# Attention chunks of 512 and 416 columns, raw loads staged in the pools of the split tiles, and a bucket prefill in halves

## The chip, the cores and the metric

The kernel runs on one core of a Trainium2 chip. The metric is the device time of that core in microseconds (us), lower is better, taken as the median of the runs. Three runs of the kernel before gave 1568.79, 1567.44 and 1567.44 us.

## What is computed

The reference has two stages, with B = 8 batches, S = 1856 rows, D = 256, 16 experts and F = 1024:

```python
scores = np.matmul(z, z.transpose(0, 2, 1)) / S        # z: 8 x 1856 x 64
x = u * np.matmul(np.maximum(scores, 0.0) ** 2, v)     # u, v: 8 x 1856 x 256
g = argmax(x @ w_group); e = argmax(x @ w_expert[g])   # 4 groups of 4 experts
out = softmax_g * softmax_e * (np.maximum(x @ w1[g, e], 0.0) @ w2[g, e])
```

The 14848 rows of x go each through one expert of 16. All is float32 to the outside; the kernel keeps float32 accuracy by splitting each matmul operand into a high and a low part of the type fp32r and adding two or three products.

## The kernel before, in words

**Attention.** For each batch the 1856 query columns are cut into four chunks, `QW` of 480, 480, 448 and 448 columns (L54). A chunk takes 15 steps, one for each 128 rows of keys (the last has 64), so there are 8 x 4 x 15 = 480 steps. In a step `scores` (L265) issues two matmuls (L272, L273) into one of three PSUM banks; ScalarE applies relu (L275) and square (L281, or L278 and L279 in steps 4 and 10); VectorE makes the high part (`ah`, L282) and the low part (`al`, L285). `attn_v` (L291) then adds six matmuls (L302, L303, L305) to two accumulators; the last step has four. Scores run `LEAD` = 5 steps ahead of `attn_v`.

**Loads.** z and v of a batch come in four blocks each. `prep_z` (L206) and `prep_v` (L236) issue the load on SyncE's queue and return a function that splits the block: a ScalarE cast (L218, L253) and a VectorE subtraction (L219, L254). The raw blocks lie in rings of their own with two buffers each (`stg` for v and the expert weights, `zr` for z); the split tiles lie in the pools `vb` (16 buffers of 128x1024) and `q` (26 buffers of 128x512), which also hold `ah` and `al`, the weights, and the hidden tiles. `prep_zm` (L224) builds the moving operand of the scores, the high part of z in 64 partitions and the low part in the other 64, with VectorE copies (L231, L232). Blocks 0 and 1 of batch 0 are loaded at the start, blocks 2 and 3 in steps 0 and 4; those of the next batch at the steps of a table `PREP` (L714), which names for each block the (chunk, step) of its load and of its split.

**Router and buckets.** `chunk_end` (L313) multiplies the accumulators by u, casts to `xh` and `xl`, writes 16-bit planes that SyncE transposes by DMA to rows (L349), and computes the router's logits with four matmuls (L357, L358), whose transpose is a DMA into `lgx` (L365). Eight steps after the end of the chunk `logits_tr` (L369) reads `lgx` on VectorE (L371); from the next step on, but not before step 42, the generator `route` (L399) is advanced by three operations a step: some 27 small VectorE operations, three small matmuls (L452 to L454), and four scatters by GpSimd (L488) that write the rows into a bucket for each expert in device memory. Before that, `prefill` (L687) has filled each expert's bucket with padding rows, one DMA of 1320 KB for each, issued on SyncE's queue at every second step from 10 to 40.

**Experts.** When all chunks are done the rows of each expert come back by transposing loads in blocks of up to 512. Phase 1 (L628 to L630) has 48 matmuls a block, phase 2 (L660, L661) makes the output, which GpSimd scatters (L674). Weights of the next expert but one are loaded in four pieces (`load_w`, L158), two at the start of a block and two behind the first splits.

The order of the instructions on each engine is made by the framework's scheduler from the program order above; a tile takes any free buffer of its pool.

Of the kernel before, what the change touches and what calls it, by code (L numbers as in the profile page):

```python
# [29 lines left out]
def tile_glu_attn_moe(  # L30
# [23 lines left out]
    QW = [480, 480, 448, 448]  # L54
    QO = [0, 480, 960, 1408]
# [10 lines left out]
    LEAD = 5  # L66
    NWARM = 32
# [3 lines left out]
    NEARLY = 2  # L71
    FRZ = min(512, min(caps[:NEARLY]))
# [13 lines left out]
    def new_vb(name):  # L86
        return sb("vb", [P, 1024], F32R, 16, name)

    def new_stg(name):
        return sb("stg", [P, 1024], F32, 2, name)  # L90

    def new_z(name):
        return sb("q", [P, 512], F32R, 26, name)

    def new_rows(name):
        return sb("rows", [P, 4, RW], I32, 3, name)
# [34 lines left out]
    whl = cst("whl", [P, ND, P], F32R)  # L131
    wh0 = cst("wh0", [P, ND, P], F32R)
# [16 lines left out]
    cst("pad", [P, 432])  # L149

    def make_router():
        nc.sync.dma_start(wrs, wr.rearrange("(c p) l -> p c l", p=P))
        for m in (whl, wh0):
            nc.gpsimd.memset(f32(m), 0.0)
            nc.vector.tensor_copy(out=m[:, :, 0:NL], in_=wrs)
        nc.vector.tensor_sub(out=whl[:, :, NL:2 * NL], in0=wrs, in1=f32(whl[:, :, 0:NL]))

    def load_w(e, wt, piece, name):  # L158

        raw = new_stg(f"raw_{name}_{piece}")  # L160
        if piece < 2:
            nc.sync.dma_start(raw, w1[ds(e, 1), piece * P:(piece + 1) * P, :].rearrange("o p f -> p (o f)"))

            def split():
                hi, lo = wt["h"][piece], wt["l"][piece]
                nc.scalar.copy(out=hi, in_=raw)
                nc.vector.tensor_sub(out=lo, in0=raw, in1=f32(hi))
        else:
            q = piece - 2
            rv = raw.rearrange("p (a d) -> p a d", d=D)  # L170
            nc.sync.dma_start(
                rv, w2[ds(e, 1), q * 4 * P:(q + 1) * 4 * P, :].rearrange("o (a p) d -> p (o a) d", p=P)
            )

            def split():
                for j in range(2):
                    t = wt["2"][2 * q + j].rearrange("p (a t d) -> p a t d", a=2, t=2)
                    nc.scalar.copy(out=t[:, :, 0, :], in_=rv[:, 2 * j:2 * j + 2, :])
                    nc.vector.tensor_sub(out=t[:, :, 1, :], in0=rv[:, 2 * j:2 * j + 2, :], in1=f32(t[:, :, 0, :]))

        return split

    def new_w(name):
        h, l = [], []
        for d in range(ND):
            h.append(new_vb(f"w1h_{name}_{d}"))
            l.append(new_vb(f"w1l_{name}_{d}"))
        return {"h": h, "l": l, "2": [new_vb(f"w2_{name}_{q}") for q in range(4)]}
# [17 lines left out]
    def prep_z(b, c):  # L206
# [29 lines left out]
    def prep_v(b, c):  # L236
        n = min(4, NK - 4 * c)
        nfull = min(n, NKF - 4 * c)
        raw = new_stg(f"vr_{b}_{c}")
# [73 lines left out]
    def chunk_end(s):  # L313
# [17 lines left out]
        lgp = sb("zr", [P, 512], F32, 2, f"lgp_{b}_{c}").bitcast(U16)[0:LP].rearrange("p (t h q) -> p t h q", t=4, q=P)  # L331
# [22 lines left out]
        def logits():  # L354
            ps = bank(ps_m, "m", f"pl_{b}_{c}")
            for d in range(ND):
                nc.tensor.matmul(ps[:, 0:w], whl[:, d, :], xh[:, d, 0:w], start=(d == 0), stop=False)  # L357
                nc.tensor.matmul(ps[:, 0:w], wh0[:, d, :], xl[:, d, 0:w], start=False, stop=(d == ND - 1))  # L358
# [22 lines left out]
        defer(s + wait, logits_tr)  # L381
        gens.append((max(s + wait + 1, 42), g))
# [13 lines left out]
    def rt_(tag, shape, name, dt=F32):  # L396
        return sb("rt_" + tag, [P] + shape, dt, 2 if tag in ("lg", "gl", "di") else 1, f"{tag}_{name}")

    def route(b, c, rows, lg, nt, part):  # L399
# [37 lines left out]
        if part:  # L437
            nc.vector.memset(oh16[part:P, nt - 1, :], 0.0)
# [60 lines left out]
    def sort_experts():  # L499
# [4 lines left out]
        sq = lambda name: sb("stg", [P, 1024], F32, 2, name)[:, 0:NE * NE].rearrange("p (a b) -> p a b", b=NE)  # L504
# [182 lines left out]
    def prefill(e):  # L687
        ins = nc.sync.dma_start(
            bucket[e * CAPB:e * CAPB + CMAX, :].rearrange("(p t) w -> p t w", p=P),
            padrow.unsqueeze(1).to_broadcast([P, CMAX // P, RW]),  # L690
# [5 lines left out]
    pz = prep_z(0, 0)  # L696
    pv = prep_v(0, 0)
# [3 lines left out]
    pz1 = prep_z(0, 1)  # L701
    pv1 = prep_v(0, 1)
    pz()
    prep_zm(0, 0)
    pv()
    make_router()
    load_ut(0, 0)
    if B == 1:
# [3 lines left out]
    pv2 = []  # L712
# [6 lines left out]
    for s in range(LEAD):  # L719
        if s == 4:  # L720
            pz1()
        scores(s)
    for s in range(NS):
        b, c, k = steps[s]
        if s == 1:
            pv1()
        if s in (0, 4):
            n0 = s // 4 + 2
            pz1 = prep_z(0, n0)
            pv2.append(prep_v(0, n0))  # L730
        if s in (2, 6):
            pz1()
        if s in (5, 9):
            pv2.pop(0)()
        if b == 0 and s >= 10 and s % 2 == 0 and s < 10 + 2 * NE:
            prefill((s - 10) // 2)
        nxt = s // NK + 1
        if k == 0:
            if nxt < B * NQ:
                load_ut(nxt // NQ, nxt % NQ)  # L740
            if b + 1 == B:
                if c == 0:
                    wts[0] = new_w("e0")
# [43 lines left out]
    for i, (e, r0, n) in enumerate(blocks):  # L787
# [6 lines left out]
        if ld is not None:  # L794
            wts[ld] = new_w(f"e{ld}")
# [27 lines left out]
    def ot(shape, name, dt=F32):  # L823
# [3 lines left out]
        if n == 1024:  # L827
            return new_stg(f"ov_{name}").rearrange("p (a b) -> p a b", b=shape[1])
# [77 lines left out]
    with tc.For_i(0, kreg) as iv:  # L906
        e_ov = nc.sync.value_load(ei[0:1, ds(iv, 1)], min_val=0, max_val=NE - 1)
        wt = new_w("ov")
# [55 lines left out]
```

## Time and profile before

| | |
|---|---|
| median of three runs | 1567.44 us (1567.44 to 1568.79) |
| the profiled execution's own time | 1568.45 us |
| its span, first to last instruction | 1566.7 us |
| TensorE (PE) busy | 1543.9 us, 99% |
| VectorE (DVE) busy | 1107.8 us, 71% |
| ScalarE (ACT) busy | 1000.4 us, 64% |
| mean granted TensorE clock | 0.995 |

Matmuls overlap in the pipeline, so a busy TensorE can still be slower than its best rate. What counts is how many matmuls a stretch holds and how far apart their starts are. Where a row has text in square brackets, it is the idle time of the engine just before the instruction, and what ended it. SPq is the issuing side of SyncE. A PEclk of 1.00 is 2.4 GHz, 0.50 is 1.2 GHz.

### The profile page before, as it was taken

The numbers are of one execution on the slowest core, as the hardware profiler recorded it, in microseconds if no ns is written. First come the engines' busy times: TensorE is split into PE (matmuls) and PEld (weight loads), VectorE is DVE, ScalarE is ACT, GpSimd is POOL, SyncE is SP. The second block draws the span as 40 slices with busy tenths as digits, with TensorE's granted clock in tenths as the row PEclk, the third lists the DMA queues.
The fourth block names the chain that finished last, engine by engine and source line by source line (L and its number), as shares of the span: only waits on it lengthen the run. The fifth ranks groups of instructions, "written<-read, shape, count | busy, mean of one in ns | idle before, by whom it ended". The sixth has DMA issues, their size and how long they took to land. (4 is left out here: it accounts for less than half of the span.)

```text
span 1566.7 us, 23639 instructions
## 1 busy us (share of the span) xinstructions
PE 1543.9 (99%) x7760; PEld 1343.0 (86%) x7760; DVE 1107.8 (71%) x2705; ACT 1000.4 (64%) x1932; POOL 293.4 (19%) x376
## 2 busy tenths in 40 slices
PE   7999999999999999999999999999999999999998
PEld 6887888888988988888889898998888888888887
DVE  6869788888788887887888656555555555555672
ACT  6877878787888887878787445444444444444432
POOL 0003212121212121212112211111221211111111
PEclk9999999999999999999999999999999999999999
DMA  8994334252443241423144344324433333433200
GB/s 252 326 272 116 88 77 107 56 137 55 99 101 87 78 112 51 109 57 96 47 113 106 100 117 126 83 82 101 107 103 96 92 104 102 96 101 103 61 21 21
DMA packets 250541, 162.83 MB, mean 104 GB/s; under 512 B 174232, under 2 KB 235676, under 8 KB 250416
## 3 DMA queue, kind: packets, MB, share of 16 engines
q1 hardware_dynamic: 238480, 130.40, 33.0%
q0 software_dynamic: 11936, 30.90, 6.1%
q8 instruction: 61, 1.00, 0.3%
q14 instruction: 64, 0.52, 0.1%
HBM read 72.50 MB, written 53.61 MB: 80 GB/s over the span
## 5 line engine op out<-in xcount | busy, mean ns | idle before, releaser
L302 PE MATMUL o<-ah,vl 128*128 128x448 f32 (+1 forms) x960 | 361.1, 376 | 3.1 <-DVE ah L282 2.4
L303 PE MATMUL o<-ah,vh 128*128 128x448 f32 (+1 forms) x960 | 359.9, 375 | 0.0
L660 PE MATMUL py<-w_e,hh 128*128 128x512 f32 x976 | 332.1, 394 | 0.0
L275 ACT ACTIVATE r<-sc 128x480 f32<-128x480 f32 (+1 forms) x480 | 259.0, 554 | 110.7 <-PE sc L273 74.6
L285 DVE TENSOR_TENSOR al<-r,ah 128x480 fp32r<-128x480 f32 (+1 forms) x448 | 285.0, 636 | 42.6 <-ACT r L279 21.3
L305 PE MATMUL o<-al,vh 128*128 128x480 f32 (+1 forms) x896 | 291.5, 377 | 5.3 <-DVE al L285 5.2
L639 DVE SCALAR_TENSOR_TENSOR hl<-ph,hh 128x512 fp32r<-128x512 f32 (+5 forms) x288 | 172.1, 605 | 114.3 <-ACT hh L633 106.4
L661 PE MATMUL py<-w_e,hl 128*128 128x256 f32 x976 | 251.9, 280 | 0.0
L633 ACT ACTIVATE hh<-ph 128x512 fp32r<-128x512 f32 (+7 forms) x288 | 153.5, 540 | 147.2 <-PE ph L630 139.4
L281 ACT ACTIVATE r<-r 128x480 f32<-128x480 f32 (+1 forms) x416 | 239.6, 591 | 5.0
L674 POOL DMA_INDIRECT out_dram<-y,meta x128 | 128.2, 1001 | 545.9 <-DVE y L672 521.6
L488 POOL DMA_INDIRECT bucket<-rows,di x128 | 136.8, 1069 | 401.3 <-DVE di L467 338.4
L628 PE MATMUL ph<-xh_m,w1l_e 128*128 128x512 f32 (+7 forms) x576 | 207.8, 361 | 0.7 <-DVE hl L639 0.7
L629 PE MATMUL ph<-xh_m,w1h_e 128*128 128x512 f32 (+7 forms) x576 | 207.8, 361 | 0.0
L630 PE MATMUL ph<-xl_m,w1h_e 128*128 128x512 f32 (+7 forms) x576 | 206.3, 361 | 0.0
L302 PEld LDWEIGHTS o<-ah,vl 128*128 128x128 f32 x960 | 181.3, 189 | 28.1 <-DVE ah L282 4.8
L660 PEld LDWEIGHTS py<-w_e,hh 128*128 128x128 f32 x976 | 175.2, 187 | 32.8
L303 PEld LDWEIGHTS o<-ah,vh 128*128 128x128 f32 x960 | 181.3, 189 | 21.2
L305 PEld LDWEIGHTS o<-al,vh 128*128 128x128 f32 x896 | 167.5, 189 | 29.6 <-DVE al L285 10.1
L282 DVE CAST ah<-r 128x480 fp32r<-128x480 f32 (+1 forms) x416 | 166.0, 401 | 35.5 <-ACT r L281 29.4
L661 PEld LDWEIGHTS py<-w_e,hl 128*128 128x128 f32 x976 | 181.5, 188 | 10.7
L272 PE MATMUL sc<-zm,z2h 128*128 128x480 f32 (+1 forms) x480 | 181.7, 381 | 3.9 <-ACT r L275 2.4
(146 smaller groups left out, 1891.6 us busy)
## 6 DMA issues: line engine op xcount, KB each, us to landing
raw_e<-in_w_dram SPq DMA_DIRECT2D x64, 512.0 KB
bucket<-padrow SPq DMA_DIRECT2D x16, 1320.0 KB
vr<-in_v_dram SPq DMA_DIRECT2D x24, 512.0 KB
ut<-in_uT_dram SPq DMA_DIRECT2D x16, 480.0 KB
ut<-in_uT_dram SPq DMA_DIRECT2D x16, 448.0 KB
zr<-in_zT_dram SPq DMA_DIRECT2D x48, 128.0 KB
vr<-in_v_dram SPq DMA_DIRECT2D x8, 256.0 KB
rows<-pl SPq DMA_TRANSPOSE x128
```

Of the source, the lines that this page charges most:

```text
L272: nc.tensor.matmul(ps[:, 0:w], z2h[:, ks], zm, start=True, stop=False)
L275: nc.scalar.activation(out=a, in_=ps[:, 0:w], func=AF.Relu, scale=1.0 / S)
L281: nc.scalar.activation(out=a, in_=a, func=AF.Square)
L285: nc.vector.tensor_sub(out=al, in0=a, in1=f32(ah))
L302: nc.tensor.matmul(o, vl[:, dsl], ah, start=(k == 0), stop=False)
L303: nc.tensor.matmul(o, vh[:, dsl], ah, start=False, stop=(k == NK - 1))
L305: nc.tensor.matmul(o, vh[:, dsl], al, start=False, stop=False)
L628: nc.tensor.matmul(o, wt["l"][d][:, fs], xh[:, d, 0:W], start=(d == 0), stop=False)
L629: nc.tensor.matmul(o, wt["h"][d][:, fs], xh[:, d, 0:W], start=False, stop=False)
L630: nc.tensor.matmul(o, wt["h"][d][:, fs], xl[:, d, 0:W], start=False, stop=(d == ND - 1))
L660: nc.tensor.matmul(py[0:m], hh[:, ts], w2t, start=(f == 0), stop=False)
L661: nc.tensor.matmul(py[0:m, 0:D], hl_[:, ts], w2t[:, 0:D], start=False, stop=(f == NF - 1))
```

## The change

Chunks get 512, 512, 416 and 416 columns. Raw blocks of z are staged in the pool `q` (27 buffers), raw v and weights in `vb` (18 buffers), so that the rings `stg` and `zr` go; `lgp` gets a buffer of its own, `rows` a fourth, `lgx` three. All z and v loads of batch 0 are issued at the start, the second half of the first z block on ScalarE's queue; for that block the operand of the scores is made directly from the raw block, half by ScalarE and half by VectorE. The router's weights are loaded at the start and split at step 8, in tiles of 48 columns, not 128. `LEAD` becomes 6, the warm-up has 40 matmuls, not 32. The prefill has 32 DMAs of half the size at steps 8 to 54, one every step and a half (`PFILL`), and routing starts at step 56 with `logits_tr` inside the generator. `PREP` splits v earlier and z later. All four pieces of an expert's weights are loaded at the start of a block.

```diff
-    QW = [480, 480, 448, 448]
-    QO = [0, 480, 960, 1408]
+    QW = [512, 512, 416, 416]
+    QO = [0, 512, 1024, 1440]
...
-    LEAD = 5
-    NWARM = 32
+    LEAD = 6
+    NWARM = 40
...
+    PFILL = [8 + 3 * i // 2 for i in range(2 * NE)]
...
-        return sb("vb", [P, 1024], F32R, 16, name)
-
-    def new_stg(name):
-        return sb("stg", [P, 1024], F32, 2, name)
+        return sb("vb", [P, 1024], F32R, 18, name)
+
+    def new_vraw(name):
+        return sb("vb", [P, 1024], F32, 18, name)
+
+    def new_zraw(name):
+        return sb("q", [P, 512], F32, 27, name)
...
-        return sb("rows", [P, 4, RW], I32, 3, name)
+        return sb("rows", [P, 4, RW], I32, 4, name)
...
-    whl = cst("whl", [P, ND, P], F32R)
-    wh0 = cst("wh0", [P, ND, P], F32R)
+    whl = cst("whl", [P, ND, LP], F32R)
+    wh0 = cst("wh0", [P, ND, LP], F32R)
...
-        zr = sb("zr", [P, 512], F32, 2, f"zr_{b}_{c}")
+        zr = new_zraw(f"zr_{b}_{c}")
         for h in range(2):
-            nc.sync.dma_start(zr[h * DQ:(h + 1) * DQ, 0:w], zT[b, :, q0:q0 + w])
+            eng = nc.scalar if first and h else nc.sync
+            eng.dma_start(zr[h * DQ:(h + 1) * DQ, 0:w], zT[b, :, q0:q0 + w])
...
+            if first:
+                zm = sb("zm", [P, 512], F32R, 2, f"zm_{b}_{c}")
+                nc.vector.tensor_sub(out=zm[DQ:P, :], in0=zr[DQ:P, :], in1=f32(z2h[DQ:P, :]))
+                nc.scalar.copy(out=zm[0:DQ, :], in_=zr[0:DQ, :])
+                zms[(b, c)] = zm
...
-        lgp = sb("zr", [P, 512], F32, 2, f"lgp_{b}_{c}").bitcast(U16)[0:LP].rearrange("p (t h q) -> p t h q", t=4, q=P)
+        lgp = sb("lgp", [P, 512], F32, 1, f"lgp_{b}_{c}").bitcast(U16)[0:LP].rearrange("p (t h q) -> p t h q", t=4, q=P)
...
-        defer(s + wait, logits_tr)
-        gens.append((max(s + wait + 1, 42), g))
+        def late():
+            logits_tr()
+            yield
+            yield from g
+
+        gens.append((max(s + wait, PFILL[-1] + 2), late()))
...
-            nc.vector.memset(oh16[part:P, nt - 1, :], 0.0)
+            if part < 64:
+                nc.vector.memset(oh16[part:64, nt - 1, :], 0.0)
+            nc.vector.memset(oh16[max(part, 64):P, nt - 1, :], 0.0)
...
-    def prefill(e):
+    def prefill(i):
+        r0, n = i // 2 * CAPB + i % 2 * (CMAX // 2), CMAX // 2
...
-        ("v", 0, (0, 1), (0, 7)), ("v", 1, (0, 9), (1, 3)), ("v", 2, (1, 5), (1, 10)), ("v", 3, (1, 12), (2, 4)),
-        ("z", 0, (1, 6), (1, 12)), ("z", 1, (2, 6), (2, 12)), ("z", 2, (3, 5), (3, 11)), ("z", 3, (3, 6), (3, 13)),
+        ("v", 0, (0, 1), (0, 6)), ("v", 1, (0, 7), (0, 12)), ("v", 2, (0, 13), (1, 4)), ("v", 3, (1, 5), (1, 10)),
+        ("z", 0, (2, 4), (2, 12)), ("z", 1, (2, 13), (3, 6)), ("z", 2, (3, 2), (3, 10)), ("z", 3, (3, 6), (3, 14)),
...
-            sp = [load_w(regs(ld)[0], wts[ld], pc, f"e{ld}") for pc in range(2)]
+            sp = [load_w(regs(ld)[0], wts[ld], pc, f"e{ld}") for pc in range(4)]
...
-                sp.append(load_w(regs(ld)[0], wts[ld], (f - 3) // 2 + 2, f"e{ld}"))
```

## Rows read from the trace of the kernel before

**Rows 1.** The page, part 1: the span, and busy time by engine.

```profile
span 1566.7 us, 23639 instructions
PE 1543.9 (99%) x7760; PEld 1343.0 (86%) x7760; DVE 1107.8 (71%) x2705; ACT 1000.4 (64%) x1932; POOL 293.4 (19%) x376
```

**Rows 2.** Windows of 50 us: length, busy time (x instructions) by engine, PEclk, DMA share, GB/s.

```profile
0.00:50.00 50.00, 41.76 (x184) 33.22 (x185) 34.81 (x67) 34.60 (x62) 3.28 (x28) 0.93 0.89 273
50.00:100.00 50.00, 50.00 (x239) 44.48 (x238) 36.21 (x97) 37.70 (x77) 1.35 (x4) 1.00 1.11 303
100.00:150.00 50.00, 46.37 (x209) 37.47 (x208) 40.79 (x131) 40.53 (x80) 13.89 (x19) 0.97 0.70 181
150.00:200.00 50.00, 50.00 (x241) 43.56 (x240) 38.88 (x110) 39.81 (x82) 10.35 (x14) 1.00 0.31 69
200.00:250.00 50.00, 48.67 (x233) 41.50 (x232) 41.17 (x115) 41.47 (x83) 10.52 (x13) 1.00 0.44 112
300.00:350.00 50.00, 50.00 (x246) 44.23 (x245) 41.91 (x120) 42.50 (x86) 7.62 (x13) 1.00 0.38 100
```

**Rows 3.** Waits, whole span: who waited for what, us in total, times, longest.

```profile
DVE lgf L371 <- DMA lgx<-lgp: 40.4, 28, 3.9
...
PE o L305 <- DVE al L285: 5.2, 8, 1.6
```

**Rows 4.** Windows of the head, cut where the granted clock changes; columns as in rows 2.

```profile
5.30:22.40 17.10, 11.66 (x44) 7.64 (x44) 11.37 (x23) 12.25 (x22) 0.00 (x0) 1.00 0.75 218
22.40:29.20 6.80, 6.06 (x15) 5.08 (x16) 5.36 (x9) 2.89 (x4) 0.08 (x1) 0.50 0.96 289
```

**Rows 5.** Timeline of the head and around 120 us: start, length, engine, line, operation.

```profile
0.81 1.22 SPq L211 DMA_DIRECT2D zr<-in_zT_dram  x2
...
1.32 3.59 PE L700 MATMUL warm_ps<-ones 128*128 128x128 bf16 x32 [1.32 <-POOL ones L114]
...
4.08 0.62 ACT L218 CAST z2h<-zr 128x512 fp32r<-128x512 f32 x1 [1.78 <-DMA zr<-in_zT_dram]
...
6.41 0.46 PE L272 MATMUL sc<-zm,z2h 128*128 128x480 f32 x1 [1.50 <-DVE zm L232]
...
9.12 8.59 SPq L241 DMA_DIRECT2D vr<-in_v_dram  x3
...
10.27 0.49 PE L302 MATMUL o<-ah,vl 128*128 128x480 f32 x1 [1.22 <-DVE ah L282]
...
14.99 1.05 ACT L253 CAST vh<-vr 128x1024 fp32r<-128x1024 f32 x1 [2.40 <-DMA vr<-in_v_dram]
...
23.14 1.17 PE L305 MATMUL o<-al,vh 128*128 128x480 f32 x2 [1.49 <-DVE al L285]
...
120.73 0.67 PE L305 MATMUL o<-al,vh 128*128 128x448 f32 x2 [1.60 <-DVE al L285]
```

**Rows 6.** Timeline of TensorE: first and last of steady rows, 448, 512, 352 columns.

```profile
300.92 0.36 PE L303 MATMUL o<-ah,vh 128*128 128x448 f32 x1
...
302.54 0.37 PE L303 MATMUL o<-ah,vh 128*128 128x448 f32 x1
...
1107.08 0.40 PE L629 MATMUL ph<-xh_m,w1h_e 128*128 128x512 f32 x1
...
1109.84 0.39 PE L629 MATMUL ph<-xh_m,w1h_e 128*128 128x512 f32 x1
...
1548.00 0.32 PE L628 MATMUL ph<-xh_m,w1l_e 128*128 128x352 f32 x1
...
1550.26 0.32 PE L630 MATMUL ph<-xl_m,w1h_e 128*128 128x352 f32 x1
```

**Rows 7.** Line 688, the prefill: SyncE's issue in ns (min/median/max), first and last start.

```profile
L688 SPq DMA_DIRECT2D bucket<-padrow x16: 588/872/4495, 22.1 to 95.8; - x16
```

**Rows 8.** Groups by shape: VectorE's two operations of a step at 448 columns.

```profile
L285 DVE TENSOR_TENSOR al<-r,ah 128x448 fp32r<-128x448 f32 x224 | 138.8, 620 | 26.5 <-ACT r L279 12.9 <-ACT r L275 4.7 <-ACT r L281 3.8
...
L282 DVE CAST ah<-r 128x448 fp32r<-128x448 f32 x208 | 82.1, 395 | 12.8 <-ACT r L281 11.8 <-issue 0.4
```

More of the change, by code (lines that the diff above doesn't have):

```diff
@@ L148, in tile_glu_attn_moe, with wr_in @@
     warm = cst("warm", [P, 1])
-    cst("pad", [P, 432])
+    cst("pad", [P, 240])
+    def wr_in():
+        nc.sync.dma_start(wrs, wr.rearrange("(c p) l -> p c l", p=P))
     def make_router():
-        nc.sync.dma_start(wrs, wr.rearrange("(c p) l -> p c l", p=P))
         for m in (whl, wh0):
@@ L158, in load_w, with split, new_w @@
     def load_w(e, wt, piece, name):
-        raw = new_stg(f"raw_{name}_{piece}")
+        raw = new_vraw(f"raw_{name}_{piece}")
+        rv = raw.rearrange("p (a d) -> p a d", d=D)
         if piece < 2:
             nc.sync.dma_start(raw, w1[ds(e, 1), piece * P:(piece + 1) * P, :].rearrange("o p f -> p (o f)"))
-            def split():
-                hi, lo = wt["h"][piece], wt["l"][piece]
+        else:
+            a0 = 4 * (piece - 2)
+            nc.sync.dma_start(rv, w2[ds(e, 1), a0 * P:(a0 + 4) * P, :].rearrange("o (a p) d -> p (o a) d", p=P))
+        def split():
+            if piece < 2:
+                hi, lo = new_vb(f"w1h_{name}_{piece}"), new_vb(f"w1l_{name}_{piece}")
+                wt["h"].append(hi)
+                wt["l"].append(lo)
                 nc.scalar.copy(out=hi, in_=raw)
                 nc.vector.tensor_sub(out=lo, in0=raw, in1=f32(hi))
[L168 to L179, printed above, removed]
-        return split
[L183 to L188, printed above, removed]
+                return
+            for j in range(2):
+                t2 = new_vb(f"w2_{name}_{2 * (piece - 2) + j}")
+                wt["2"].append(t2)
+                t = t2.rearrange("p (a t d) -> p a t d", a=2, t=2)
+                nc.scalar.copy(out=t[:, :, 0, :], in_=rv[:, 2 * j:2 * j + 2, :])
+                nc.vector.tensor_sub(out=t[:, :, 1, :], in0=rv[:, 2 * j:2 * j + 2, :], in1=f32(t[:, :, 0, :]))
+        return split
+    def new_w():
+        return {"h": [], "l": [], "2": []}
     deferred = []
@@ L238, in prep_v @@
         nfull = min(n, NKF - 4 * c)
-        raw = new_stg(f"vr_{b}_{c}")
+        raw = new_vraw(f"vr_{b}_{c}")
         rv = raw.rearrange("p (k d) -> p k d", d=D)
@@ L356, in logits @@
             for d in range(ND):
-                nc.tensor.matmul(ps[:, 0:w], whl[:, d, :], xh[:, d, 0:w], start=(d == 0), stop=False)
-                nc.tensor.matmul(ps[:, 0:w], wh0[:, d, :], xl[:, d, 0:w], start=False, stop=(d == ND - 1))
+                nc.tensor.matmul(ps[0:LP, 0:w], whl[:, d, :], xh[:, d, 0:w], start=(d == 0), stop=False)
+                nc.tensor.matmul(ps[0:LP, 0:w], wh0[:, d, :], xl[:, d, 0:w], start=False, stop=(d == ND - 1))
             for t0, t1, q in ((0, w // P, P), (w // P, nt, part)):
@@ L695, in tile_glu_attn_moe @@
     nc.scalar.activation(out=warm, in_=warm, func=AF.Exp)
-    pz = prep_z(0, 0)
-    pv = prep_v(0, 0)
+    pz, pv = [prep_z(0, 0, first=True)], [prep_v(0, 0)]
     wps = bank(ps_m, "m", "warm_ps")
@@ L700, in tile_glu_attn_moe @@
         nc.tensor.matmul(wps[:, 0:P], ones, ones, start=True, stop=True)
[L701 to L706, printed above, removed]
+    for c in range(1, NQ):
+        pz.append(prep_z(0, c))
+        pv.append(prep_v(0, c))
+        if c == 1:
+            wr_in()
+    pz.pop(0)()
     load_ut(0, 0)
@@ L719, in tile_glu_attn_moe @@
     for s in range(LEAD):
+        if s == 1:
+            pv.pop(0)()
         if s == 4:
-            pz1()
+            pz.pop(0)()
         scores(s)
@@ L725, in tile_glu_attn_moe @@
         if s == 1:
[L726 to L730, printed above, removed]
+            pv.pop(0)()
         if s in (2, 6):
-            pz1()
+            pz.pop(0)()
         if s in (5, 9):
-            pv2.pop(0)()
-        if b == 0 and s >= 10 and s % 2 == 0 and s < 10 + 2 * NE:
-            prefill((s - 10) // 2)
+            pv.pop(0)()
+        if s == 8:
+            make_router()
+        for i in range(2 * NE):
+            if PFILL[i] == s:
+                prefill(i)
         nxt = s // NK + 1
```

22 lines of the change are left out of this document (11 added, 11 removed).

## The prediction

> **What bounds the kernel now.** I read the page first. TensorE is busy for 1543.9 of 1566.7 us [rows 1], so it is the bound, and a faster VectorE or ScalarE is worth nothing unless TensorE waits for it. But a busy share hides a slow clock and small gaps, so I then cut the span into windows of 50 us and read how many matmuls each holds [rows 2]. Steady attention has 241 and 246; the first window has 184, of which 32 are the warm-up [rows 5]; 100 to 150 us has 209, and 200 to 250 us has 233. So time is lost in three places, all in the first 250 us, and what is left of the attention stage and all of the expert stage run without a gap that I could take out. The list of waits says the same: in sum the matmul that reads `al` waits for VectorE for 5.2 us in 8 places, which is the longest entry of TensorE [rows 3]. Third I read the head in windows cut where the granted clock changes [rows 4] and in its timeline [rows 5].
>
> **A matmul's price.** From first to last start there are 8 intervals in 1.62 us at 448 columns, 12 in 2.76 us at 512, 14 in 2.26 us at 352 [rows 6]: 0.2025, 0.230 and 0.161 us. They lie on a line of 0.00043 us a column. On it 480 columns cost 0.216 us and 416 cost 0.189 us.
>
> **The head, as it is.** In 0 to 50 us the 152 matmuls behind the warm-up are worth 152 x 0.216 = 32.9 us; 17.1 us are lost. Of these
> - 6.4 us lie before the first score, which starts at 6.41 [rows 5].
> - From 6.41 to the first `attn_v` at 10.27 are eight score matmuls, 1.7 us; 2.1 us are lost.
> - 5.30 to 22.40 holds 44 matmuls [rows 4], so 36 from 10.27 on, worth 7.8 of 12.1 us; 4.3 us are lost. SyncE stands in a load of v from 9.12 for 8.59 us, since the two raw buffers are full; ScalarE waits 2.40 us for a block of v at 14.99, and behind that wait stands the split of z block 1, which the next scores need [rows 5].
> - 22.40 to 29.20 is at a granted clock of 0.50, the 1.2 GHz level, after TensorE had idled again and again from 6 us on; 15 matmuls are worth 3.2 of 6.8 us [rows 4], 3.6 us are lost, the wait of 1.49 us for `al` at 23.14 among them [rows 5].
> - 0.7 us behind that.
>
> **The change, part by part.**
>
> *Widths.* Each chunk keeps its 118 attention and 4 router matmuls. A wide and a narrow one cost 0.230 + 0.189 = 0.419 us, today's pair 0.216 + 0.2025 = 0.419 us. Cost 0. The 352-column row lies on the line, so no floor stands at 416. On ScalarE and VectorE counts stay and the columns sum to the same; a chunk of 512 needs one plane copy for each half where 480 needs two. Cost 0, gain hidden.
>
> *All first loads at once.* This takes away the block of 8.59 us on SyncE and the wait of 2.40 us behind it. Blocks of z and v are then issued in the order of their use, each some 0.6 us of issue (1.22 us for two, [rows 5]), all eight by about 11 us; the last are wanted at step 9. What is late next is ScalarE and VectorE: until then ten steps of at most 1.0 us each (VectorE, below) and some 5 us of splits stand against ten steps of 8 x 0.230 = 1.84 us, 15 against 18 us, so they keep up on the mean, though not at each step. So I take out most of 4.3 and, as TensorE no longer idles in pieces, most of the 3.6 us: 6.5 us. Bounds: 2 us (the splits still collide) and 8.6 us (all, with the 0.7).
>
> *First operand direct, ScalarE's queue, warm-up, LEAD.* The operand is ready one VectorE operation after the cast, not three, which is up to 0.9 us earlier; the second half of z, issued on another queue, may land 0.6 us earlier, or up to 0.9 us later if it queues behind ScalarE's table load. Eight more warm-up matmuls of 3.59/32 = 0.11 us [rows 5] end at 5.8 us, so the first score can't start before. With a sixth step of scores ahead, ScalarE has one more relu before the steady order. Gain 0.5 us for start, 0.5 for the rest; bounds -1 and 2. Head together: -7.5 us, bounds -1 and -10.6.
>
> *Prefill in 32 halves.* Now 16 DMAs, 21.6 MB, are asked for in steps 10 to 40, some 52 us, and are still being issued at 95.8 us [rows 7]; 50 to 100 us moves 303 GB/s [rows 2], so the rings are full and every load of z and v queues behind padding; SyncE itself stands up to 4.5 us in one issue [rows 7]. Halves every 1.5 steps, 2.6 us, ask for 676 KB/2.6 us = 260 GB/s, under that rate, and end at step 54, about 105 us. On SyncE 32 issues of 0.59 (the least) to 0.87 us (the median) cost 19 to 28 us where 16 cost 14; the transposes for rows and logits are queued behind them, which no one needs before step 56. Cost on the path 0.
>
> *Routing from step 56, `lgp` and more buffers.* In 100 to 150 us 32 matmuls are missing, 32 x 50/241 = 6.6 us; one wait there is for `al` at 120.73, 1.60 us [rows 5], and the clock falls again (0.97 in the mean). VectorE is held in order by `lgf`, which waits for the transpose of the logits: 40.4 us in 28 waits, up to 3.9 us [rows 3]; behind it stand `ah` and `al`, and TensorE waits for those. For the first chunks that transpose has long landed when routing starts at 56. The same 27 small operations for each of the first chunks come later by 14 steps, again at three a step, until about step 110; so VectorE is as full as now, with TensorE one step better buffered. Gain 5 us, bounds 0 and 6.6. From step 110 on `lgf` comes eight steps behind the chunk as before, and waits as before.
>
> *200 to 250 us.* Missing are 8 matmuls, 1.7 us [rows 2]; the longer lead should cover more than half. Gain 1 us, bounds -4 (a loss, by more of such waits in the narrow chunks) and 1.7.
>
> *At no cost.* Weight pieces all at the start of a block, router tiles of 48 columns, the second memset of VectorE in narrow chunks (one less in wide ones), two pools for raw tiles: hidden under a TensorE that doesn't wait; if the pools were full, a load would stand in SyncE as at 9.12 us now. By count `vb` needs 16 + 2 of 18, `q` at most 25 of 27.
>
> **The sum.** The profiled execution took 1568.45 us. Less 7.5, 5 and 1 is 1554.95. It stands 1.0 us over the median of 1567.44, within the spread of the three runs. Forecast: 1555 us; its own range is 1549.5 to 1560.5.
>
> **Rivals.**
> 1. *The head is mended, the middle isn't.* Routing at three operations a step meets the splits of the next batch's v in steps 66 to 85, and VectorE's pile-up only moves. For it: the demand is unchanged. Against it: the late loads are gone. 1568.45 - 7.5 = 1561 us. Chance 0.18.
> 2. *Stalls move in the head too.* ScalarE, not the loads, spaces the first steps; only 2 us are gained: 1566.5 us. For it: ScalarE and VectorE are busy over 11 of the 17 us from 5.3 on [rows 4]. Against it: its longest idle time there is a wait for a load. Chance 0.10.
> 3. *Halves are slow.* If halves moved only 218 GB/s, as the first 17 us did [rows 4], 21.6 MB would take 99 us, not the 83 us of the schedule; loads and transposes would queue 16 us late as today, and the 5 us, the 1 us and some 4 of the head's 7.5 would not come: 1565 us. The Trainium skill speaks for this one: DMA: Bandwidth & Descriptors, Rules for kernel authors, wants at least 1 MiB in a DMA for full bandwidth, and halves have 0.64. The trace shows no prefill of that size, so it neither agrees nor differs. Chance 0.05.
> 4. *Narrow chunks become VectorE's.* A step of 448 columns costs VectorE 0.620 + 0.395 = 1.015 us [rows 8], 15.2 us a chunk; it is busy 41.9 of 50 us [rows 2], so 20.4 of a chunk's 24.3, 5.2 of them not by step. At 416 columns TensorE needs 15 x 8 x 0.189 = 22.7 us; VectorE at most the same 20.4, and with 1.4 us of the `lgf` wait 21.8, which is 96%. With three splits of z put into the last narrow chunk it can pass 22.7, from where each further operation is on the path. At 1.0 us in each of 16 narrow chunks the loss is 16 us: 1568.45 - 13.5 + 16 = 1571 us, slower. Against it: VectorE's time falls with the columns, and wide chunks have 27.6 us for it to catch up. Chance 0.12.
>
> **Chances and range.** The forecast has 0.55. Measurement can tell about 0.2%, 3.1 us, from no change. Faster: the forecast, rival 1, and the better end of rival 2, 0.76. Same: the rest of 2 and rival 3, 0.12. Slower: rival 4, 0.12. The range of 1549 to 1566.5 holds all but rival 4 and the ends.
>
> **What would show it.** Right: about 40.4/0.230 = 175 matmuls behind the 40 warm-ups in 0 to 50 us, where there are 152 now; no SyncE block near 9 us; a granted clock of 1.00 from 6 us on; starts 0.230 and 0.189 us apart; the prefill ending near 105 us. A window of 50 us wholly in wide chunks holds 217 matmuls, one in narrow chunks 264. Wrong: a new row of waits for `al` in the narrow chunks, windows beyond 250 us that stay five or more under what their widths give, or a clock at 0.50 in the head.

## The result

The changed kernel is slower. Its median is 1587.82 us (four runs, 1586.04 to 1591.96) beside 1567.97 us (four runs, 1567.44 to 1568.79) for the kernel before: ratio 1.013, 95% interval 1.0109 to 1.0151. Predicted was 1555 us, between 1549 and 1566.5. The profiled execution took 1588.44 us, 20.0 us more than that of before.

The page of the changed kernel, parts 1 and 5: the span, busy time by engine, and one of TensorE's groups with the idle time ahead of it.

```profile
span 1586.7 us, 23447 instructions
PE 1547.3 (98%) x7768; PEld 1335.2 (84%) x7768; DVE 1100.5 (69%) x2672; ACT 997.0 (63%) x1885; POOL 300.2 (19%) x344
...
L316 PE MATMUL o<-al,vh 128*128 128x512 f32 (+1 forms) x896 | 292.0, 377 | 12.1 <-DVE al L296 11.7
```

VectorE and ScalarE have fewer instructions and less busy time than in [rows 1], and TensorE has eight more, the warm-up. So none of the three got more work that matters. TensorE waits more: 39.4 us of the span are not busy, 22.8 before. Where, is told by windows again: a stretch is worth the matmuls that it holds. The changed kernel (columns as in rows 2):

```profile
0.00:50.00 50.00, 36.81 (x149) 26.42 (x150) 26.94 (x47) 27.84 (x47) 2.48 (x26) 0.86 0.98 302
...
100.00:150.00 50.00, 45.48 (x213) 40.51 (x212) 35.44 (x87) 36.69 (x75) 0.48 (x2) 0.93 0.96 274
150.00:800.00 650.00, 638.07 (x3041) 544.03 (x3041) 528.11 (x1523) 524.04 (x1008) 138.25 (x159) 0.99 0.32 86
```

And the kernel before in the long stretch:

```profile
150.00:800.00 650.00, 648.11 (x3102) 564.17 (x3101) 536.88 (x1549) 533.65 (x1061) 127.74 (x174) 1.00 0.34 85
```

Before 150 us the changed kernel has 149 + 239 + 213 less 40 warm-ups, 561 matmuls, where the kernel before has 600 [rows 2]; from 150 to 800 us it has 3041 against 3102. At 650/3102 = 0.21 us each, 39 and 61 matmuls are 8.2 and 12.8 us, together 21: the 20 us, as nearly as counts tell. Behind 800 us both kernels take 0.190 us a matmul, so the expert stage loses nothing.

Part of the loss is the clock. In the mean of 0 to 50, 100 to 150 and 200 to 250 us the granted clock is 0.86, 0.93 and 0.93, in the kernel before 0.93, 0.97 and 1.00 [rows 2]. The third window of the changed kernel:

```profile
200.00:250.00 50.00, 47.98 (x237) 43.81 (x236) 38.49 (x117) 38.28 (x77) 11.84 (x15) 0.93 0.43 115
```

That is 50 x (0.14 + 0.07 + 0.07) = 14 us of full clock lost against 5, so up to 9 of the 20 us. This is an estimate from these rows, and an upper bound, since an idle TensorE loses nothing to its clock.

Three places stand out in the trace.

**The head.** Timeline of the changed kernel, from 10 us:

```profile
10.57 0.18 DVE L162 CAST whl<-wrs 128x40 fp32r<-128x40 f32 x1 [7.91 <-DMA wrs<-in_wr_dram]
...
10.88 0.69 DVE L227 TENSOR_TENSOR zm<-zr,z2h 64x512 fp32r<-64x512 f32 x1
...
11.62 1.65 PE L283 MATMUL sc<-zm,z2h 128*128 128x512 f32 x3 [5.86 <-DVE zm L227]
```

The first score starts at 11.62 us, at 6.41 before [rows 5]. VectorE stood for 7.91 us ahead of the first operation on the router's weights, and `zm`, which TensorE needs, is behind it. The code asks for that operation at step 8; the scheduler put it first. Why it did so is not shown: the load itself is issued at 4.15 us, and in the kernel before at 4.53 us, where `zm` comes first all the same. The three matmuls of 1.65 us run at the pace of half the clock (starts some 0.46 us apart, 0.228 is the price in experiment 8), and the granted clock of the first 50 us is 0.86. The Trainium skill (Perfetto Trace Analysis, Tensor Engine Instruction (MATMUL, LD_WEIGHTS)) calls VectorE and ScalarE strict first-in first-out; the rows agree: `zm` starts only when the router's operation has run.

**Around 119 us.** Waits of the changed kernel from 100 to 150 us, and its SyncE queue there:

```profile
DVE lgf L382 <- DMA lgx<-lgp: 7.0, 1, 7.0
...
PE o L316 <- DVE al L296: 4.0, 1, 4.0
```

```profile
96.99 7.48 SPq L708 DMA_DIRECT2D bucket<-padrow  x6
...
110.68 8.95 SPq L360 DMA_TRANSPOSE rows<-pl  x4
119.73 1.20 SPq L376 DMA_TRANSPOSE lgx<-lgp  x1
```

`lgf` holds VectorE for 7.0 us, because the transpose of the logits is issued only at 119.73, behind halves of the prefill and four transposes that took 8.95 us. The last half of the prefill is issued at 132.6 us, not at 105:

```profile
L708 SPq DMA_DIRECT2D bucket<-padrow x32: 588/1088/2602, 15.3 to 132.6; - x32
```

**Every batch turn**, where one batch follows another: the first product with v of batches 3, 4 and 5 starts at 246, 354 and 461 us. Two windows of the changed kernel at such a turn:

```profile
250.00:300.00 50.00, 48.04 (x210) 37.31 (x209) 37.99 (x112) 39.59 (x72) 9.92 (x10) 1.00 0.26 66
...
450.00:500.00 50.00, 47.99 (x213) 37.12 (x213) 41.78 (x116) 41.23 (x75) 8.93 (x9) 1.00 0.32 91
```

TensorE is idle for 2 us of each, with a clock of 1.00, and so at 350 and 550 us (209 and 218 matmuls); the kernel before has no idle time in three of these four and 0.2 us in the one from 550. From 200 to 250 us there are another 2 us, and behind a wait of 1.8 us at 238 us the clock falls (the 0.93 above). SyncE's waits of line 252, the load of v, in 200 to 800 us, in the changed kernel:

```profile
SPq L252 <- PE o L314: 26.1, 4, 9.6
...
SPq L252 <- PE o L316: 13.8, 5, 3.2
SPq L252 <- PE sc L284: 4.4, 4, 1.2
```

and of the same load in the kernel before:

```profile
SPq L241 <- DVE vl L254: 20.7, 7, 6.8
```

Before, a load of v mostly waits until a raw block has been split. Now it waits for a matmul, 44 us in 13 waits. L314 and L316 read the split tiles of v, so the slot, a buffer of the pool, that the load needs holds a split tile which TensorE still reads (L284 reads none of them; its 4.4 us are only put down to it). So blocks land late, and ScalarE stands for them; its waits from 200 to 800 us:

```profile
ACT vh L264 <- DMA vr<-in_v_dram: 9.4, 9, 1.3
```

The kernel before has no such wait there. What ScalarE does for TensorE is behind it in order. TensorE's waits from 150 to 800 us, in the changed kernel:

```profile
PE sc L283 <- ACT r L286: 6.1, 9, 1.8
PE o L316 <- DVE al L296: 4.9, 12, 0.6
```

and in the kernel before:

```profile
PE o L305 <- DVE al L285: 1.6, 4, 0.6
```

The splits also come closer together. ScalarE's splits of v at one turn, changed kernel:

```profile
450.89 1.05 ACT L264 CAST vh<-vr 128x1024 fp32r<-128x1024 f32 x1 [0.34 <-DMA vr<-in_v_dram]
...
454.21 1.05 ACT L264 CAST vh<-vr 128x1024 fp32r<-128x1024 f32 x1
...
458.93 0.83 ACT L264 CAST vh<-vr 128x768 fp32r<-128x768 f32 x1
...
465.42 1.05 ACT L264 CAST vh<-vr 128x1024 fp32r<-128x1024 f32 x1 [1.23 <-DMA vr<-in_v_dram]
```

The first three of these are 3.3 and 4.7 us apart; before the fourth, ScalarE stands for 1.23 us, and TensorE's waits of this turn follow it, from 469 to 477 us. In the kernel before:

```profile
425.51 1.05 ACT L253 CAST vh<-vr 128x1024 fp32r<-128x1024 f32 x1
...
432.90 1.04 ACT L253 CAST vh<-vr 128x1024 fp32r<-128x1024 f32 x1
```

The next two start at 439.4 and 445.8 us. The four are 6.4 to 7.4 us apart, three of them ahead of the turn at 445.0 us.

### The profile page after: what moved, and what is told of

It is laid out like the page before. It is cut to its first block, busy times and chain, and to the rows that moved or that the text cites. A ratio compares the mean times of both kernels' runs of the same rounds, so it can differ in the third digit from the quotient of the medians.

```text
span 1586.7 us, 23447 instructions
## 1 busy us (share of the span) xinstructions
PE 1547.3 (98%) x7768; PEld 1335.2 (84%) x7768; DVE 1100.5 (69%) x2672; ACT 997.0 (63%) x1885; POOL 300.2 (19%) x344
## 5 line engine op out<-in xcount | busy, mean ns | idle before, releaser
L313 PE MATMUL o<-ah,vl 128*128 128x416 f32 (+1 forms) x960 | 361.4, 377 | 5.3 <-DVE ah L293 4.5
L314 PE MATMUL o<-ah,vh 128*128 128x416 f32 (+1 forms) x960 | 358.5, 373 | 0.0
L286 ACT ACTIVATE r<-sc 128x512 f32<-128x512 f32 (+1 forms) x480 | 259.0, 554 | 129.8 <-PE sc L284 81.9
L296 DVE TENSOR_TENSOR al<-r,ah 128x512 fp32r<-128x512 f32 (+1 forms) x448 | 286.3, 639 | 33.5 <-ACT r L290 23.7
L316 PE MATMUL o<-al,vh 128*128 128x512 f32 (+1 forms) x896 | 292.0, 377 | 12.1 <-DVE al L296 11.7
L507 POOL DMA_INDIRECT bucket<-rows,di x128 | 142.9, 1116 | 531.1 <-DVE di L486 393.8
L292 ACT ACTIVATE r<-r 128x512 f32<-128x512 f32 (+1 forms) x416 | 238.9, 592 | 5.0
L693 POOL DMA_INDIRECT out_dram<-y,meta x128 | 133.8, 1046 | 535.4 <-DVE y L691 507.5
L316 PEld LDWEIGHTS o<-al,vh 128*128 128x128 f32 x896 | 167.5, 190 | 40.7 <-DVE al L296 20.4
L314 PEld LDWEIGHTS o<-ah,vh 128*128 128x128 f32 x960 | 182.2, 190 | 19.7
L293 DVE CAST ah<-r 128x512 fp32r<-128x512 f32 (+1 forms) x416 | 167.6, 406 | 41.8 <-ACT r L292 41.2
L283 PE MATMUL sc<-zm,z2h 128*128 128x512 f32 (+1 forms) x480 | 182.7, 384 | 13.0 <-ACT r L286 7.0
```

The costliest lines, as they stand in the source:

```text
L283: nc.tensor.matmul(ps[:, 0:w], z2h[:, ks], zm, start=True, stop=False)
L286: nc.scalar.activation(out=a, in_=ps[:, 0:w], func=AF.Relu, scale=1.0 / S)
L292: nc.scalar.activation(out=a, in_=a, func=AF.Square)
L296: nc.vector.tensor_sub(out=al, in0=a, in1=f32(ah))
L313: nc.tensor.matmul(o, vl[:, dsl], ah, start=(k == 0), stop=False)
L314: nc.tensor.matmul(o, vh[:, dsl], ah, start=False, stop=(k == NK - 1))
```

## The experiments

Each was timed beside the kernel before; medians of that were 1568.3 to 1568.7 us. The theory was that **slots** are scarce, since raw blocks lie in the pools of the split tiles. Rivals: **narrow chunks** fall behind VectorE (rival 4 of the prediction), and the **head**.

### 1. The router's weights loaded beside their split

```diff
-        if c == 1:
-            wr_in()
...
+            wr_in()
             make_router()
```

> The changed kernel with the load of the router's weights moved from the start to step 8, beside their split. Theory H (at the start VectorE holds the first operand and the low part of z behind the router's split, which waits for its small load until 10.6 us): the first score starts at 5.5 to 6.5 us, not at 11.6, and the time falls by 4 to 8 us, to 1580 to 1584; the windows behind 200 us keep their losses. Rival (the head is bound by the first loads of z and v, all asked for at once): the first score still starts behind 9 us, and the time stays within 2 us of 1588.

1594.17 us, ratio 1.0168 (1.015 to 1.0186): worse, outside of both expectations. Timeline:

```profile
6.12 0.99 PE L283 MATMUL sc<-zm,z2h 128*128 128x512 f32 x3 [0.36 <-DVE zm L227]
...
13.13 0.79 PE L313 MATMUL o<-ah,vl 128*128 128x512 f32 x1 [4.32 <-DVE ah L293]
...
20.72 0.18 DVE L162 CAST whl<-wrs 128x40 fp32r<-128x40 f32 x1 [3.87 <-DMA wrs<-in_wr_dram]
```

The first score starts at 6.12, as the theory of the head wanted, but the first product with v only at 13.13 (10.27 before, 16.91 in the changed kernel): ScalarE stands for 2.41 us for the second block of v, and the scores' work is behind that split. The router's load, issued at 14.58 us behind the first loads of z, v and u, holds VectorE at 20.72. The first 50 us hold 144 matmuls, where the changed kernel has 149. Mending one such wait uncovers the next.

### 2. The widths of before in the changed kernel

```diff
-    QW = [512, 512, 416, 416]
+    QW = [480, 480, 448, 448]
```

> The changed kernel with chunks of 480, 480, 448, 448 columns, all else kept. Theory W (rival 4 of the prediction, narrow chunks leave VectorE too little time): the waits for al at the turn of each batch go, 12 to 17 us come back, 1571 to 1576. Theory S (raw blocks in the pools of the split tiles make the splits of v wait and then come in a heap at the turn): the heap stays, 1585 to 1591.

1587.63 us, 1.012 (1.0103 to 1.0137): no difference from the changed kernel. TensorE is idle for 11.7 us from 150 to 800 us, 11.9 in the changed kernel, and waits of 1.3 to 1.4 us for `al` stand at 254, 361, 469 and 577 us. So the narrow chunks of rival 4 don't make the stalls at the turns.

### 3. Rings of their own for the raw tiles

```diff
-        return sb("vb", [P, 1024], F32, 18, name)
+        return sb("stg", [P, 1024], F32, 2, name)
...
-        return sb("q", [P, 512], F32, 27, name)
+        return sb("zr", [P, 512], F32, 2, name)
...
-        lgp = sb("lgp", [P, 512], F32, 1, f"lgp_{b}_{c}")...
+        lgp = sb("zr", [P, 512], F32, 2, f"lgp_{b}_{c}")...
```

> The changed kernel with raw blocks in rings of their own again (two buffers for v and weights, two for z, shared with the logits' planes; vb 16, q 26). Theory S: the splits of v spread over some 12 steps before the turn of a batch, as in the kernel before; each turn from batch 2 on loses under 1.5 us where it now loses about 4; 10 to 15 us come back, 1573 to 1578, with the head still near 21 us lost. Theory W: the turns keep their losses, 1585 to 1591.

1572.89 us, 1.0029 (1.0017 to 1.004): 14.9 us back with nothing else undone. `q` and `vb` have 26 and 16 buffers again. Its long window:

```profile
150.00:800.00 650.00, 644.71 (x3102) 554.59 (x3101) 538.74 (x1554) 535.80 (x1024) 132.20 (x160) 1.00 0.32 86
```

61 matmuls more than the changed kernel, 12.8 of the 14.9 us; ScalarE never stands there for a block of v to land; and line 252 waits no more for a matmul; its longest entry is

```profile
SPq L252 <- DVE vl L265: 9.4, 8, 1.5
```

The head changes too, though nothing of its loads was touched. Timeline:

```profile
5.11 0.69 DVE L227 TENSOR_TENSOR zm<-zr,z2h 64x512 fp32r<-64x512 f32 x1 [2.45 <-ACT z2h L224]
...
9.91 0.18 DVE L162 CAST whl<-wrs 128x40 fp32r<-128x40 f32 x1 [0.49 <-DMA wrs<-in_wr_dram]
```

The router's operation is behind `zm` again, and the first score starts at 5.86 us. So it stood first only with the shared pools and all first loads together; with the shared pools alone (experiment 10) `zm` starts at 6.16 us and the router's operation at 9.54.

The experiment gives back both pools and the logits' planes at once. By SyncE's waits it is `vb` that matters: in the changed kernel line 217, the load of z, waits for 7 us from 200 to 800 us, line 252 for 44.

### 4. The preparation steps of before in the changed kernel

The two lines of `PREP` as in the kernel before.

> The changed kernel with the table of load and split steps of the kernel before. Theory S: the splits of z spread over the batch again, those of v stay in a heap since the pool lets none go earlier; 2 to 6 us come back, 1582 to 1586. Theory T (the table alone makes the heap): the turns lose no more than before, 10 to 15 us come back, 1573 to 1578.

1582.6 us, 1.0092 (1.0076 to 1.0109): 5.2 us back. Loads of v and splits are spread wider in this table, and line 252 waits 32 us for matmuls, not 44.

### 5. Both: rings and preparation steps

> The changed kernel with pools of its own for the raw tiles (as in the run with split pools) and with the order of preparation steps of before; widths, first loads, prefill and routing stay as changed. If the lack of free slots is what bunched the splits at each batch turn, both edits mend the same thing and do not add: 1568 to 1573 us, about the 1572.9 of the pools alone. If the order of the steps has a cost of its own, they add: 1567 to 1569 us (1587.8 - 15 - 5). Against it, what remains of the loss would then be the head and the stretch from 100 to 150 us.

1575.32 us, 1.0044 (1.0027 to 1.0061). They don't add, and the time is above both expectations: with rings of their own the old table is 2.4 us worse than the new one, but the intervals overlap. So the table of before only eased the lack of slots.

### 6. And the first loads in the order of before

```diff
-    for c in range(1, NQ):
-        pz.append(prep_z(0, c))
-        pv.append(prep_v(0, c))
+    pz.append(prep_z(0, 1))
+    pv.append(prep_v(0, 1))
...
+        if s in (0, 4):
+            pz.append(prep_z(0, s // 4 + 2))
+            pv.append(prep_v(0, s // 4 + 2))
```

> As the run before it, with the first loads in the order of the kernel before: two blocks and nothing else at the start, the next two at steps 0 and 4, the router's weights and their split behind the first product with v. If the head was what the change lost after the batch turns (in the changed kernel 21.1 us of TensorE's first 50 are not matmuls at their rate, in the kernel before 13.8), this gives 5 to 8 us back: 1562 to 1567 us, below the kernel before. If all loads at once are no worse in the head than two by two, within 2 us of the run before it.

1573.64 us, 1.0031 (1.0021 to 1.0041): 1.7 us, not 5 to 8, and the intervals overlap. The first 150 us hold 587 matmuls instead of 581. All at once is no gain; two by two is hardly better in this surrounding.

### 7. And the prefill whole, the routing from step 42

```diff
-    PFILL = [8 + 3 * i // 2 for i in range(2 * NE)]
+    PFILL = [10 + 2 * i for i in range(NE)]
...
-        gens.append((max(s + wait, PFILL[-1] + 2), late()))
+        defer(s + wait, logits_tr)
+        gens.append((max(s + wait + 1, PFILL[-1] + 2), g))
```

> As the run before it, with prefill in 16 whole blocks at steps 10 to 40 and routing from step 42 as in the kernel before. What is left of the change: widths, first stacked tile direct, second half of the block on ScalarE's queue, 40 warm-up matmuls, lead 6. If halves and later routing pay by themselves, this is slower than the run before it by 2 to 5 us; if the stall at 120 us only changed its place, it is the same within 1.5 us. Theory: same; in the changed kernel the stall is there still (4.4 us at 119 us).

1568.74 us, 1.0003 (0.9994 to 1.0013): 4.9 us faster, where the same was expected. Halves and later routing together cost here, they don't pay.

### 8. The widths alone in the kernel before

```diff
-    QW = [480, 480, 448, 448]
-    QO = [0, 480, 960, 1408]
+    QW = [512, 512, 416, 416]
+    QO = [0, 512, 1024, 1440]
```

> The kernel before with chunks of 512, 512, 416, 416 and nothing else. If widths cost nothing, as the run with 480 and 448 in the changed kernel says, 1567 to 1570 us, the same as before. If narrow chunks fall behind VectorE or ScalarE in a kernel whose splits are not late, 1572 us or more.

The second memset that a last tile of 32 rows needs came with it. 1560.65 us, 0.9947 (0.993 to 0.9963): **7.7 us faster**, outside of both expectations. No later run beat it. The long window:

```profile
150.00:800.00 650.00, 648.74 (x3138) 568.63 (x3137) 542.03 (x1547) 535.24 (x1034) 124.65 (x150) 1.00 0.34 87
```

36 matmuls more in the same time, with the same busy time of TensorE: the matmuls themselves are cheaper. Taking every start-to-start interval of that stretch which is within 12 ns of columns/2.4 + 16, the means are 217.1 ns (480 columns, 1505 intervals) and 204.0 (448, 1439) in the kernel before, 227.8 (512, 1547) and 187.7 (416, 1430) here. Less the columns at 2.4 GHz that is 17.1, 17.3, 14.5 and 14.4 ns. A pair costs 415.5 instead of 421.1 ns; 1952 pairs (8 batches, 4 chunks, 122 matmuls, halved) make 10.9 us. The run has 13 matmuls fewer in its first 150 us, 2.7 us, which leaves 8.2.

### 9. Lead 5 and 32 warm-ups, added to experiment 7

> The run that has pools, preparation steps, first loads, prefill and routing as before, and now lead 5 and 32 warm-up matmuls as before too. What is left of the change: widths, first stacked tile direct with its second half on ScalarE's queue, weight pieces and small buffers. That run has a stall of about 1.5 us at every batch turn (al waits at 233, 356, 460, 564 and 668 us), which the kernel before with the new widths alone (1560.65) does not have. If a sixth step of scores ahead makes them, 1559 to 1563 us. If the parts called free make them, 1567 to 1570 us as without this edit.

1563.55 us, 0.9971 (0.996 to 0.9983): 5.2 us faster than experiment 7, just above the first band. Lead and warm-up were not taken apart. What is left of the change here (widths, first tile direct, weight pieces, router tiles and buffers) is 2.9 us from the widths alone.

### 10. The shared pools alone in the kernel before

```diff
-        return sb("vb", [P, 1024], F32R, 16, name)
+        return sb("vb", [P, 1024], F32R, 18, name)
...
-        return sb("stg", [P, 1024], F32, 2, name)
+        return sb("vb", [P, 1024], F32, 18, name)
...
-        zr = sb("zr", [P, 512], F32, 2, f"zr_{b}_{c}")
+        zr = sb("q", [P, 512], F32, 27, f"zr_{b}_{c}")
```

> The kernel before, with one edit alone: raw tiles of v and weights out of the pool of the split v tiles (18), raw tiles of z out of the pool of the split z tiles (27), routing's logits in a tile of their own. If lack of free slots is the cause of the stalls at the batch turns in the changed kernel, this shows them alone: 1574 to 1584 us, with stalls at 250, 350, 450, 550 and 650 us. If slots are not the cause and split pools helped the changed kernel for another reason, 1566 to 1571 us.

1578.49 us, 1.0066 (1.0049 to 1.0083): 9.8 us slower, and loads of v that wait for matmuls again:

```profile
SPq L241 <- PE o L305: 22.4, 5, 5.1
...
SPq L241 <- PE o L303: 15.5, 4, 4.1
SPq L241 <- PE sc L273: 7.0, 4, 2.3
```

ScalarE stands for blocks of v again, 6.0 us in 9 waits from 200 to 800 us. Of the 9.8 us, 25 matmuls, 5.3 us, are missing from 150 to 800 us, and 22 ahead of it. TensorE's waits of over 1 us lie at 251, 463 and 570 us; those expected at 350 and 650 are absent. So the shared pools are shown as the cause from both sides, by taking them out of the one kernel and putting them into the other. How a late block reaches TensorE is read from the traces.

### 11. Halves and later routing beside the new widths

> The kernel before with the new widths (1560.65 alone) and with the prefill in 32 halves and routing behind it, as the change has them. The pair of runs that differed in this alone gave 1573.6 with and 1568.7 without. If that is this part's own cost, 1563 to 1567 us. If it costs only beside lead 6 and the other parts, 1559 to 1562 us.

1562.2 us, 0.9961 (0.9947 to 0.9975): 1.5 us over the widths alone, and the intervals overlap. Waits from 100 to 150 us:

```profile
DVE lgf L373 <- DMA lgx<-lgp: 2.5, 1, 2.5
```

The wait for the logits is smaller than the 7.0 us of the changed kernel, and the gain of 5 us still doesn't come. The last half is issued nearly as late as there (129.7 us), while the queues' share from 50 to 100 us is 0.73: it isn't bandwidth that makes the halves late, SyncE stands for 7.1 us in a load of u whose buffer isn't free.

### 12. The first tile direct beside the new widths

> The kernel before with the new widths (1560.65 alone) and with the first stacked tile made directly and the second half of the first z block on ScalarE's queue. Predicted was a gain of 0.5 us, bounds -1 and 2. If the first score starts earlier and the rest of the head follows: 1558 to 1560.5 us. If the first product with v sets the head, which waits for the split of v: the same as without it within 1 us.

1560.87 us, 0.9948 (0.9932 to 0.9965): nothing. The first score starts at 5.79 instead of 7.09 us, but its matmuls start some 0.46 us apart, the pace of half the clock (0.43 without it); the first product with v comes at 10.51 us, 10.8 without it.

### 13. Lead 6 and 40 warm-ups beside the new widths

> The kernel before with the new widths (1560.65 us alone) and with lead 6 and 40 warm-up matmuls. If a sixth step of scores ahead makes the stall of about 1.5 us at each batch turn: 1564 to 1568 us, with stalls near 250, 356, 460, 564 and 668 us. If it needs another part of the change to do so, 1559 to 1562 us.

1569.73 us, 1.0009 (0.9999 to 1.0018): 9.1 us lost, more than either theory said. Timeline at one turn:

```profile
351.57 0.63 ACT L278 ACTIVATE ah<-r 128x512 fp32r<-128x512 f32 x1
352.09 0.90 ACT L362 COPY lgp<-pl 48x768 uint16<-48x768 uint16 x2
352.87 0.65 ACT L281 ACTIVATE r<-r 128x512 f32<-128x512 f32 x1
353.40 0.63 ACT L279 ACTIVATE r<-r 128x512 f32<-128x512 f32 x1
...
354.07 0.69 DVE L285 TENSOR_TENSOR al<-r,ah 128x512 fp32r<-128x512 f32 x1 [2.73 <-ACT r L279]
...
354.81 0.74 PE L305 MATMUL o<-al,vh 128*128 128x512 f32 x2 [1.12 <-DVE al L285]
```

In step 4 ScalarE makes both squares. Another step's square comes between them here and in experiment 8; with lead 6 the copy of the logits does too, where with lead 5 it follows behind. So `al` is late, and TensorE waits 1.12 us. This is the pattern at 248, 353, 458, 562 and 666 us. From 150 to 800 us 23 matmuls, 4.8 us, are missing against experiment 8, and 17 before.

### 14. Rings and lead 5 as the only edits to the changed kernel

> The changed kernel with two edits: split pools (alone 1572.9 us) and lead 5 with 32 warm-up matmuls. If the lead costs 5 us wherever the pools are split, as it did with seven other edits undone: 1566 to 1569.5 us, about the kernel before. If it cost there because the preparation steps were those of before, 1571 to 1575 us.

1571.39 us, 1.0021 (1.0012 to 1.0031): 1.5 us from the lead, and the intervals overlap, with a wait of TensorE of 1.1 to 1.2 us that begins at 351, 456, 560 and 665 us, where the rings alone had less. In experiment 9 the same edit gave 5.2 us beside the old table. That the lead and the table of preparation steps are fitted to each other would explain it, but first loads and prefill differ there too, so it isn't shown.

### 15. The widths of before in experiment 9

> The run with everything undone but widths, first tile, weight pieces and buffers (1563.55 us), now with chunks of 480, 480, 448, 448. If 480 and 448 columns cost some 3 ns a matmul more than their columns, and stalls no longer hide it: 1570 to 1574 us. If the gain of the widths in the kernel before came from how its splits fall, 1562 to 1566 us.

1569.12 us, 1.0006 (0.9996 to 1.0016): 5.6 us slower than with 512 and 416, just under the expected band. The head of this run holds more (610 matmuls before 150 us, 589 with the new widths, 4.4 us), so the price of 448 and 480 columns is there. In experiment 2 it was hidden: that run has 11 matmuls fewer than the changed kernel from 150 to 800 us, but 23 more, 4.8 us, before.

### 16. Chunks of 512, 512, 512 and 320 in the kernel before

> The kernel before with chunks of 512, 512, 512, 320 and nothing else. In the expert stage a matmul of 512 columns takes some 14 ns beyond its columns at 2.4 GHz, of 320 and 384 13.3, of 480 17, of 448 20. If this price of the width is the whole gain, 1558 to 1562 us, as with 416. If a narrow chunk falls behind VectorE or ScalarE (a step of 320 columns takes TensorE 8 x 0.147 = 1.18 us), 1564 us or more, with waits for al in every fourth chunk.

1570.85 us, 1.0019 (1.0009 to 1.0029), with 512 columns as cheap as in experiment 8 (227.96 ns). TensorE's waits from 150 to 800 us:

```profile
PE o L305 <- DVE al L285: 6.0, 6, 2.1
PE sc L272 <- ACT r L275: 1.5, 7, 0.3
```

The narrow chunk comes last in its batch, and the stalls lie at every turn (230, 337, 444, 549, 653 us). Ahead of the longest, 2.1 us, VectorE stands for 2.65 us for `lgf` and then splits a block of v. So what rival 4 of the prediction feared, VectorE falling behind in narrow chunks, shows itself at 320 columns; at 416 (experiment 8) TensorE has two waits of 0.7 and 0.4 us in this stretch.

## Why the prediction was wrong

What each edit is worth, taking them out of the changed kernel in this order: 1587.8 us, less 14.9 (rings), plus 2.4 (table), less 1.7 (first loads), 4.9 (prefill and routing), 5.2 (lead and warm-up) and 2.9 (the rest) is 1560.65, the widths alone, which is 7.7 under the kernel before. Medians of the kernel before alone differ by 1.2 us from one set of runs to another, so the small ones are rough (the 2.4 and 1.7 lie within overlapping intervals), and another order gives other shares (lead and table above all).

- ***At no cost*, the two pools: this step failed most.** It counted 16 + 2 of 18 buffers and stopped there, and it looked for the danger in SyncE's head of 9.12 us only. The count is that of the kernel before, 16 and a ring of 2. But a raw block in a ring of two waits for a split, and one in the shared pool waits for the last matmul that reads an older tile; ScalarE then stands for it, and TensorE for ScalarE. What stood at no cost is 14.9 us, 12.8 of them behind 150 us (experiment 3), and 9.8 us alone (experiment 10).
- ***All first loads at once*, -6.5 us: wrong, no gain or a small loss.** SyncE's block is gone as predicted, but behind the warm-ups the first 50 us hold 109 matmuls, where 175 were forecast and 152 stood before. The router's operation took the block's place on VectorE. With rings of their own that wait is gone, all loads still issued at once, and the first 50 us hold 116 (experiment 3); with the first loads of before in addition they hold 121 (experiment 6). So the spacing of the first loads was not what held the head back. What does is not shown; lead 6 with its warm-ups is part of it (135 with lead 5, experiment 9, against 116, experiment 7).
- ***Routing from step 56*, -5 us: wrong.** It took the transpose of the logits to have "long landed". It depends on SyncE, where the halves end at 132.6 us and not 105, and VectorE stood for it for 7.0 us. With the halves, beside the new widths (experiment 11), the step gains nothing; the two were not taken apart.
- ***Prefill in 32 halves*, cost 0:** the least issue time was right (588 ns), the median is 1088 ns, not 872, and the end was off by 28 us, since SyncE waits in order for other loads between the halves (11.3 us for a buffer of u, before 105.6 us).
- ***LEAD*, -0.5, and *200 to 250 us*, -1: wrong.** A sixth step of scores is no more cushion. It moves the squares against the chunk's copies, and with the eight warm-ups cost 9.1 us in experiment 13, 5.2 in 9 and 1.5 in 14.
- ***First operand direct*, 0.5:** experiment 12 measures 0.
- ***Widths*, cost 0: wrong, by a gain.** The prices were read from a few rows, and 480 and 416 columns from a line between them: 0.216 + 0.2025 against 0.230 + 0.189. Means over 1400 and more intervals differ from these by 1 to 2.2 ns each, and that is 10.9 us over 1952 pairs. The 0.230 is from 12 intervals of the expert stage [rows 6]; with the same selection the mean there, too, is 227.3 ns at 512 columns. This hides how much the rest of the change loses: 27 us, not 20.
- **Rivals.** The second had the sign of the head (stalls only move) and was given 0.10; the third foresaw late transposes, but by the rate of the halves; none had a price for slots. The fourth, the only slower one, named the wrong mechanism. What the prediction offered as a sign of being wrong did come true: windows beyond 250 us under their widths (209 and 210 matmuls, where even one wholly in wide chunks holds 217), and a clock of 0.50 in the head.

Left open: why 480 and 448 columns cost 3 ns more than 512 and 416; which tile holds each slot at a turn; why the shared pools and the early loads together put the router's operation first. The chunk's offset is not the reason for the first: the matmuls of a chunk read their tiles from column 0 whatever the offset, and the expert stage, which has no chunks, has the same order (below).

## What to carry to other kernels

A pool shared by raw and split tiles can have enough buffers by count and still stall: look at what each load would wait for, a split or the last reader of an old tile. Where a scheduler makes the order of an in-order engine, the place of an operation in the program doesn't tell what it stands in front of: the router's split, asked for at step 8, ran ahead of the first score's operand in one kernel and behind it in another. Look in the trace. And a price that is multiplied by thousands is taken as a mean over hundreds of intervals for each size, not from a few rows and a line.

## What the hardware showed that was not expected

- The start-to-start price of a matmul beyond its columns depends on the width: 14.4 ns at 416 and 14.5 at 512, 17.1 at 480 and 17.3 at 448 columns (means above), at the full clock. In phase 1 of the expert stage of the kernel before, with the same selection, it is 13.3 ns at 320, 13.5 at 384, 14.0 at 512, 16.7 at 480 (47 intervals) and 19.9 at 448 (141).
- A small load among large ones (the router's weights, 20 KB), issued near 4 us, was there for VectorE only at 10.57 us in the changed kernel, and at 9.48 us in the kernel before.
